# Top-k attention and a channel mix on one core: both passes over a batch's heads in the same order, and the last store on another queue

## The chip, the core and the metric

The kernel runs on one core of one Trainium2 chip. The metric is device time in microseconds (us) of one execution; less is better. A core has five engines that run their own instruction streams: TensorE (PE, matrix products and turns of tiles), VectorE (DVE), ScalarE (ACT), GpSimd (POOL) and SyncE (SP, which here only issues transfers). They wait for each other through semaphores. Transfers are done by 16 DMA engines; an engine's queue only issues them, in order, so that a transfer that has to wait holds up all that stand behind it on that queue.

## The reference

```python
# q, k, v: [8 batches, 8 heads, 576 tokens, 64]
scores = matmul(q, k.T) / sqrt(64)
kth = 32nd largest score of each row
scores = where(scores >= kth, scores, -1e9)
attn = exp(scores - max); attn /= sum(attn) + 1e-9
x = (attn @ v), heads side by side           # [8, 576, 512]
x_prev = x, one token later, zero in front
xk = mu_k * x + (1 - mu_k) * x_prev
xr = mu_r * x + (1 - mu_r) * x_prev
k = relu(xk @ w_k)                           # 512 -> 1024
out = sigmoid(xr @ w_r) * ((k * k) @ w_v)    # 1024 -> 512
```

## The kernel before

**Work.** Attention goes by pairs of heads (`hp`, four to a batch) and by tiles of 128 rows of scores: tile `i` from 0 to 7 of a pair alternates between its two heads over the first 512 tokens, tile 8 holds the last 64 tokens of both heads. That is 36 tiles a batch and 288 in all. A tile is scored on TensorE, copied to `sc` by ScalarE, searched for its 32nd largest value by VectorE (`cand`, `top`) with help of ScalarE and GpSimd (`sg`), masked (`E`), turned (`et`, `el`) and multiplied with `v` ("weigh", L1047 and L1048). After each four tiles (and after tile 8) the inverse row sums are spread by GpSimd into the single buffer `ri` (L1061), turned by TensorE (L1065), copied back by ScalarE (L1071), and VectorE "places" the weighed rows times `ri` in `xT` (L1078, L1080). The channel mix goes through the 4608 tokens in 19 chunks of `SIZES`: GpSimd and ScalarE make `xd`, `xm`, `xh`, `xl` from `xT`, TensorE multiplies them with `w_k` ("hidden"), `w_r` ("gate") and `w_v` ("value", all of them L687 to L689), and the result in `eb` is stored (L1217).

**Passes.** A batch is visited in parts, so that the mix of its first tokens can begin early: the first pass takes tiles 0 to 3 of each pair, the second tiles 4 to 8 (the last batch has three passes: 0 to 3, 4 to 7, 8). `visits()` lists them. Where two neighbouring visits are of the same pair, they are made one. Each visit loads the rest of the keys (`tl`), the queries (`qn`) and the values (`v`, `vr`, `vr8`), each of `tl`, `v`, `vr` and `vr8` into one buffer, so that a load waits for the last reader of the visit before. The keys of the first 512 tokens (`K`) are loaded and turned on a pair's first visit and kept: `K` has `1 + HOLD` = 4 buffers.

**Order.** Nothing is ordered by hand. Every step becomes an operation with a due time (`key`: the number of its tile, or the chunk's start, plus a constant from `OFF`) and a rough cost; `Plan.run` goes forward in a time of its own and lets the engine that can start first take, of the operations that are nearly ready, the one with the least due time. The order that comes out is fixed in the program. A small change of the graph can so exchange operations far from it. The weights are loaded as 20 blocks of 512 KB (L1246; those of `w_k` into `stage`, four buffers) in the time of the first 20 tiles, and unpacked by ScalarE and VectorE (L1247 to L1263), also between tiles.

**End.** After its last operation each engine reads a flag (L1339), branches past a second, exact version of the kernel that does not run here (L1345), and goes through closing semaphores (L1345, L1408). SyncE closes one semaphore for each lane of its transfers.

Of the kernel before, what the change touches and what calls it, by code (L numbers as in the profile page):

```python
# [26 lines left out]
HP = H // 2  # L27
# [16 lines left out]
           store=4.14, w=20.061, wabs=-2.342, wclamp=0.949, wshift=-6.042, wsign=-2.057, wexp=-2.168, wfine=1.502, whi=3.775, wmul=5.552,  # L44
           wsub=-10.606, wlo=3.473, spread=1.98, sliver=-2.472, low=4.289, lowt=-10.047, lowr=-8.942, lowc=-1.374)
CANDS, BESTS = 0.043, -0.709
LAG, STEP, WAT, WSTEP, GATE, VALUE, PACE = 10.811, 15.812, 2.487, 0.785, 7.769, 14.051, -2.0
HOLD = 3
HALVES = range(4), range(4, 9)
EDGE = {B - 1: (range(4), range(4, 8), range(8, 9))}  # L50

# [1 line left out]
def visits():  # L53

    vs = []
    for b in range(B):
        for k, part in enumerate(EDGE.get(b, HALVES)):
            for hp in range(HP)[::-1] if k % 2 else range(HP):
                if vs and vs[-1][:2] == (b, hp):
                    part = range(vs.pop()[2][0], part[-1] + 1)  # L60
                vs.append((b, hp, part))
                part = EDGE.get(b, HALVES)[k]
    return vs


VISITS = visits()
SIZES = [256] * 15 + [192, 256, 192, 128]
EVAC = 0, "et"
# [9 lines left out]
LWAT, LWSTEP = -2.585, 1.51  # L78
LAG0, LAG1 = 8.92, 22.884
WPE = 12  # L80
HEAD, TAIL = {}, {}
EARLY, LATE = 48, 252
LOOK = 16
WHOLE = "tk", "tq", "tr", "turn", "turni"
FULL = "sc", "K", "kd", "et", "el", "sg", "qs", "xm", "r", "eb", "lb", "ri"
MORE = dict(xh=2, xl=2, et=3, top=3, el=2, qn=2, K=1 + HOLD)

# [79 lines left out]
class Plan:  # L167
# [8 lines left out]
    def buf(self, name):  # L176
        return Buf(self.kinds[name])
# [225 lines left out]
def topk_attention_channel_mix(ctx: ExitStack, tc: tile.TileContext, q, k, v, mu_k, mu_r, w_k, w_v, w_r, out):  # L403
    nc = tc.nc
# [281 lines left out]
    def three(ps, sh, sl, mh, ml, first, last):  # L686
        return [nc.tensor.matmul(ps, lhsT=sh, rhs=mh, start=first, stop=False),  # L687
                nc.tensor.matmul(ps, lhsT=sh, rhs=ml, start=False, stop=False),  # L688
                nc.tensor.matmul(ps, lhsT=sl, rhs=mh, start=False, stop=last)]  # L689
# [160 lines left out]
    def new_batch(g):  # L850
        x = g.two.tile([128, HP, 1 + S], F32, name="xT")
        nc.gpsimd.memset(x[:, :, 0:1], 0.0)
        return x

    def attend(plan, visits, X, pair_sums):
        PE_, ACT, DVE, POOL, SP = plan.LANES
        starts = [0]
# [4 lines left out]
        units, seen, held = {}, None, {}  # L862

        for p, (b, hp, part) in enumerate(visits):
            P = Env()
            P.first = part[0]
# [5 lines left out]
            if fresh:  # L872
                P.kn, P.K = buf("kn"), buf("K")
            if any(x[:2] == (b, hp) for x in visits[p + 1:p + 1 + 2 * HOLD]):
                held[b, hp] = P.K
# [220 lines left out]
    def mixes(plan, xT, ready, tiles_all, X):  # L1096
        PE_, ACT, DVE, POOL, SP = plan.LANES
# [8 lines left out]
        chunks, t0 = [], 0  # L1106
        for size in SIZES:
            pieces, o = [], t0
            while o < t0 + size:
                b, s = divmod(o, S)  # L1110
                m = min(S - s, t0 + size - o)
# [7 lines left out]
        def piece(name, key, n, f, reads, writes):  # L1119
            cost = n  # L1120
            after = [last[0]] if last[0] else []
            o = plan.op(PE_, name, key, cost, cost + 180, f, reads=reads, writes=writes, mode="R", after=after, pace=min(key + PACE, tiles_all))
            last[0] = o
            return o

        at, size = 0, 0
        for c, (pieces, n, rows) in enumerate(chunks):
# [15 lines left out]
            for which in (0, 1):  # L1143
                xh, xl = C.x[which] = buf("xh"), buf("xl")
                k0 = key(0 if which == 0 else GATE)
                for i in range(2):
# [11 lines left out]
                    def add(i=i, xm=xm, offs=offs):  # L1158
# [4 lines left out]
                            reads=[xm], writes=[(xh, i)])  # L1163
                    plan.op(POOL, "xl" + "kr"[which], k0, 143 + 2.13 * 2 * n, 200 + 2.13 * 2 * n, lambda i=i, xm=xm, xh=xh, xl=xl, n=n: nc.gpsimd.tensor_sub(xl.t[:, 2 * i:2 * i + 2, :n], xm.t[:, :, :n], xh.t[:, 2 * i:2 * i + 2, :n].bitcast(F32)),
                            reads=[xm, (xh, i)], writes=[(xl, i)])
            hh, hl = buf("hh"), buf("hl")
            xh, xl = C.x[0]
            for f in range(0, NFB, 2):
# [6 lines left out]
                k1 = key(f + 1)  # L1175

                def relu(ph=ph, rr=rr, n=n):
# [7 lines left out]
                        reads=[rr, (hh, f)], writes=[(hl, f)], after=X.staged)  # L1185
            xh, xl = C.x[1]
            C.g = {}
            for t in range(0, n, 128):
                m = min(128, n - t)
                G = C.g[t] = Env()  # L1190
# [5 lines left out]
                k1 = key(GATE + 1 + t // 64)  # L1196
# [5 lines left out]
            for t in range(0, n, 128):  # L1202
                m = min(128, n - t)
                G = C.g[t]
                pv = buf("rot")
                for part in range(4):
                    def val(t=t, m=m, part=part, pv=pv, hh=hh, hl=hl):
                        return [y for f in range(part * NFB // 4, (part + 1) * NFB // 4) for y in three(pv.t[:m], hh.t[:, f, t:t + m], hl.t[:, f, t:t + m], wv[0][:, f, :], wv[1][:, f, :], f == 0, f == NFB - 1)]
                    piece("value", key(VALUE + t // 32 + part), 6 * 231, val, [(hh, 2 * part), (hl, 2 * part), (X.w["v"], (2 * part, 0)), (X.w["v"], (2 * part + 1, 0))], [pv])
                k1 = key(VALUE + 3 + t // 32)  # L1210
                if c == len(chunks) - 1:
                    plan.op(DVE, "scaled", k1, 586, 694, lambda G=G, m=m: nc.vector.scalar_tensor_tensor(G.e.t[:m], G.e.t[:m], 2.0, G.l.t[:m], op0=OP.subtract, op1=OP.mult), reads=[G.l], writes=[G.e])
                    plan.op(DVE, "gated", k1, 586, 694, lambda G=G, m=m, pv=pv: nc.vector.scalar_tensor_tensor(G.e.t[:m], G.e.t[:m], -1.0, pv.t[:m], op0=OP.mult, op1=OP.mult), reads=[pv], writes=[G.e])
                else:
                    plan.op(DVE, "scaled", k1, 586, 694, lambda G=G, m=m, pv=pv: nc.vector.scalar_tensor_tensor(pv.t[:m], G.l.t[:m], -1.0, pv.t[:m], op0=OP.mult, op1=OP.mult), reads=[G.l], writes=[pv])
                    plan.op(DVE, "gated", k1, 586, 694, lambda G=G, m=m, pv=pv: nc.vector.scalar_tensor_tensor(G.e.t[:m], G.e.t[:m], 2.0, pv.t[:m], op0=OP.subtract, op1=OP.mult), reads=[pv], writes=[G.e])
                plan.op(SP, "store", k1, 600, 2500, lambda G=G, m=m, t=t, rows=rows: nc.sync.dma_start(rows[t:t + m], G.e.t[:m]), reads=[G.e])  # L1217

    def weights(plan, X):
        PE_, ACT, DVE, POOL, SP = plan.LANES  # L1220
# [47 lines left out]
    def pipeline(stack):  # L1268
# [37 lines left out]
        def graph():  # L1306
            plan = Plan()
            for name, (tiles, banks, free) in made.items():
                plan.kind(name, len(tiles), banks, free)
                plan.kinds[name].tiles = tiles  # L1310
            X = Env()
            X.ranks, X.least, X.mu = plan.buf("ranks"), plan.buf("least"), plan.buf("wmu")
            def consts_in():
                return [nc.vector.tensor_copy(X.ranks.t[:, :9], ranks_i), nc.vector.memset(X.ranks.t[:, 9:10], -SCALE), nc.vector.memset(X.ranks.t[:, 10:11], BELOW)]
            plan.op("DVE", "ranks", -9, 250, 350, consts_in, writes=[X.ranks])
            plan.op("SP", "mu", 1.0, 1100, 2900, load_mu, writes=[X.mu])
            plan.op("DVE", "nmu", 3.0, 80, 183, lambda: nc.vector.tensor_scalar(nmu, mu, -1.0, 1.0, op0=OP.mult, op1=OP.add), writes=[X.mu])
            weights(plan, X)
            mixes(plan, *attend(plan, VISITS, X, pair_sums), X)
            return plan  # L1320
# [24 lines left out]
    with tc.If(again > 0):  # L1345
        with tc.For_i(0, B, 1) as b, ExitStack() as stack:
# [7 lines left out]
            rows = out[bass.ds(b, 1)].rearrange("o s d -> (o s) d")  # L1354
# [57 lines left out]
```

## Time and profile before

| | |
|---|---|
| median of 3 runs | 1287.63 us (1286.77 to 1289.1) |
| the profiled execution | 1288.26 us |
| its span, first to last instruction | 1286.4 us |
| TensorE busy | 1212.4 us, 94% |
| VectorE busy | 1139.6 us, 89% |
| ScalarE busy | 1115.1 us, 87% |
| GpSimd busy | 987.3 us, 77% |
| DMA, mean | 47 GB/s, 60.08 MB |
| granted TensorE clock, mean | 0.973 |

A share over the whole span hides the stages. The granted clock is 1.00 for nearly all of the time after the first 150 us (2.4 GHz) and 0.50 (1.2 GHz) in stretches before that, in one near 220 us and in one near the end of the attention.

### The profile page before, as it was taken

The numbers are of one execution on the slowest core, as the hardware profiler recorded it, in microseconds if no ns is written. First come the engines' busy times: TensorE is split into PE (matmuls) and PEld (weight loads), VectorE is DVE, ScalarE is ACT, GpSimd is POOL, SyncE is SP. The second block draws the span as 40 slices with busy tenths as digits, with TensorE's granted clock in tenths as the row PEclk, the third lists the DMA queues.
The fourth block names the chain that finished last, engine by engine and source line by source line (L and its number), as shares of the span: only waits on it lengthen the run. The fifth ranks groups of instructions, "written<-read, shape, count | busy, mean of one in ns | idle before, by whom it ended". The sixth has DMA issues, their size and how long they took to land.

```text
span 1286.4 us, 29892 instructions
## 1 busy us (share of the span) xinstructions
PE 1212.4 (94%) x9196; PEld 927.0 (72%) x9196; DVE 1139.6 (89%) x6219; ACT 1115.1 (87%) x2446; POOL 987.3 (77%) x885
## 2 busy tenths in 40 slices
PE   5876899999999999999999999999999999998996
PEld 2444676877777777777677777777778777776885
DVE  5999999999999999999999999999899999997110
ACT  5887898999999999999999989998989899997441
POOL 2559986887779868978698878887979778888583
PEclk8987799999999999999999999999999999999999
DMA  6233012111220112011211121112110111011000
GB/s 171 97 95 90 28 36 61 37 30 35 57 53 25 49 45 61 21 44 39 67 30 35 29 70 39 33 27 63 42 49 21 50 41 47 16 40 31 24 18 24
DMA packets 122090, 60.08 MB, mean 47 GB/s; under 512 B 99648, under 2 KB 114752, under 8 KB 121920
## 3 DMA queue, kind: packets, MB, share of 16 engines
q1 hardware_dynamic: 121376, 57.95, 16.9%
q8 instruction: 75, 1.23, 0.4%
q14 instruction: 95, 0.78, 0.2%
q10 hardware_dynamic: 544, 0.13, 0.0%
HBM read 48.60 MB, written 9.44 MB: 45 GB/s over the span
## 4 chain that ended last, share of the span: by engine, by line
PE 57%; ACT 18%; DVE 14%; POOL 4%; issue 1%; DMA 1%; SPq 0%; POOLq 0%; ACTq 0%; DVEq 0%
PE rot L687 10%; PE rot L689 9%; PE rot L688 9%; PE ps L1047 7%; PE rot L1017 6%; PE ps L971 6%; ACT sg L1001 3%; DVE cand L981 3%; ACT sc L976 3%; ACT se L1009 3%; DVE E L1012 3%; ACT et L1019 2%; DVE top L1004 2%; PE ps L967 2%; PE ps L1048 2%; PE ps L958 1%
## 5 line engine op out<-in xcount | busy, mean ns | idle before, releaser
L1003 POOL TENSOR_TENSOR sg<-sc,sg 128x576 f32<-128x576 f32 x288 | 409.9, 1425 | 183.3 <-ACT sg L1001 181.4
L981 DVE MAX8 cand<-sc 128x8 f32<-128x82 f32 (+1 forms) x2016 | 390.9, 232 | 11.7 <-ACT sc L976 10.5
L1001 ACT ACTIVATE sg<-sc,seen 128x576 f32<-128x576 f32 x288 | 226.4, 786 | 9.7 <-DVE seen L993 8.0
L1012 DVE SCALAR_TENSOR_TENSOR E<-sc,seen,se 128x576 f32<-128x576 f32 x288 | 231.2, 803 | 1.3 <-PE rot L1017 0.6
L1009 ACT ACTIVATE se<-sc,seen 128x576 f32<-128x576 f32 x288 | 217.6, 756 | 12.6 <-DVE E L1012 6.2
L1004 DVE MAX8 top<-sg 128x8 f32<-128x576 f32 x288 | 215.9, 750 | 12.5 <-POOL sg L1003 12.2
L976 ACT ACTIVATE sc<-ps 128x576 f32<-128x576 f32 x288 | 185.6, 657 | 33.6 <-PE ps L971 13.1
L1017 PE MATMUL rot<-ident,E 128*128 128x128 f32 x1152 | 182.9, 283 | 16.0 <-DVE E L1012 5.5
L1019 ACT ACTIVATE et<-rot 128x512 f32<-128x512 f32 x288 | 174.2, 606 | 13.1 <-PE rot L1017 10.6
L687 PE MATMUL rot<-xh,wk 128*128 128x256 f32 (+2 forms) x608 | 180.3, 297 | 2.1 <-ACT et L1019 1.1
L983 DVE MAX8 top<-cand 128x8 f32<-128x56 f32 x864 | 180.0, 208 | 2.4
L1017 PEld LDWEIGHTS rot<-ident,E 128*128 128x128 f32 x1152 | 132.7, 143 | 68.5 <-issue 7.8
L1047 PEld LDWEIGHTS ps<-et,v 128*64 128x64 f32 x2560 | 130.6, 140 | 58.6 <-ACT el L1028 20.0
L1047 PE MATMUL ps<-et,v 128*64 128x128 f32 (+1 forms) x2560 | 166.5, 274 | 4.3 <-ACT el L1028 3.5
L689 PE MATMUL rot<-xh,wk 128*128 128x256 f32 (+2 forms) x608 | 170.2, 280 | 0.0
L688 PE MATMUL rot<-xl,wk 128*128 128x256 f32 (+2 forms) x608 | 170.1, 280 | 0.0
L971 PE MATMUL ps<-K,qs 64*128 64x512 f32 x512 | 150.3, 665 | 0.0
L687 PE MATMUL rot<-wv,hh 128*128 128x512 f32 (+1 forms) x296 | 127.1, 429 | 2.5 <-ACT et L1019 2.3
L687 PEld LDWEIGHTS rot<-xh,wk 128*128 128x128 f32 x608 | 115.8, 191 | 8.3 <-ACT et L1019 2.3
L689 PE MATMUL rot<-wv,hl 128*128 128x512 f32 (+1 forms) x296 | 117.2, 396 | 0.0
L688 PE MATMUL rot<-wv,hh 128*128 128x512 f32 (+1 forms) x296 | 116.4, 393 | 0.0
L986 DVE MATCH_REPLACE8 cand<-top,cand 128x56 f32<-128x56 f32 x576 | 116.0, 201 | 0.0
(114 smaller groups left out, 2758.5 us busy)
## 6 DMA issues: line engine op xcount, KB each, us to landing
v<-in_v SPq DMA_DIRECT2D x59, 256.0 KB, 2.8
out<-eb SPq DMA_DIRECT2D x35, 256.0 KB, 2.2
kn<-in_k SPq DMA_DIRECT2D x64, 128.0 KB, 2.8
qn<-in_q SPq DMA_DIRECT2D x126, 64.0 KB, 2.1
stage<-in_moe_w_k SPq DMA_DIRECT2D x8, 512.0 KB, 5.5
xT<-in_moe_w_v SPq DMA_DIRECT2D x8, 512.0 KB, 3.7
xT<-in_moe_w_r SPq DMA_DIRECT2D x4, 512.0 KB, 6.4
tl<-in_k SPq DMA_DIRECT2D x118, 16.0 KB, 2.0
```

The lines of the kernel that those rows point to most:

```text
L687: return [nc.tensor.matmul(ps, lhsT=sh, rhs=mh, start=first, stop=False), nc.tensor.matmul(ps, lhsT=sh, rhs=ml, start=False, stop=False), ...
L688: nc.tensor.matmul(ps, lhsT=sh, rhs=ml, start=False, stop=False),
L689: nc.tensor.matmul(ps, lhsT=sl, rhs=mh, start=False, stop=last)]
L971: return [nc.tensor.matmul(ps[h].t, lhsT=qs.t[w, c * 128:(c + 1) * 128], rhs=P.K.t[w], start=True, stop=True) for h, w in enumerate(ws)]
L981: lambda T=T, c=c: nc.vector.max(T.cand.t[:, 8 * c:8 * c + 8], T.sc.t[:, CUTS[c]:CUTS[c + 1]]), reads=[T.sc], writes=[(T.cand, c)])
L1001: lambda T=T, sn=sn: nc.scalar.activation(T.side.t, T.sc.t, AF.Sign, bias=sn(T, 1), scale=-BELOW, accum_out=T.top.t[:, TOPK:TOPK + 1]),
L1003: plan.op(POOL, "below", n, 1375, 1430, lambda T=T: nc.gpsimd.tensor_mul(T.side.t, T.sc.t, T.side.t), reads=[T.sc], writes=[T.side])
L1004: plan.op(DVE, "eighth", n, 660, 754, lambda T=T: nc.vector.max(T.top.t[:, 24:32], T.side.t), reads=[T.side], writes=[(T.top, 3)])
L1009: plan.op(ACT, "exps", n, 667, 754, lambda T=T, pe=pe, sn=sn: nc.scalar.activation(pe.t, T.sc.t, AF.Exp, bias=sn(T, 0), scale=SCALE), read ...
L1012: lambda T=T, U=U, pe=pe, sn=sn: nc.vector.scalar_tensor_tensor(T.e(), T.sc.t, sn(T, 2), pe.t, op0=OP.is_ge, op1=OP.mult, accum_out=U.rs.t ...
L1017: return [nc.tensor.transpose(pt.t[:, c * 128:(c + 1) * 128], E.t[:, o + c * 128:o + (c + 1) * 128], ident) for c in range(NKC)]
L1047: return [*[nc.tensor.matmul(pa[hs[j]], lhsT=vs[j][:, c, :], rhs=ms[c][j], start=(c == 0), stop=False) for c in range(NKC) for j in range(2)],
```

## The change

`visits()` gets a flag `BACK`, False. Before, the second pass went through the pairs backwards (0 1 2 3, then 3 2 1 0), so that the visit at the turn was one visit of nine tiles; now both passes go 0 1 2 3. The turned keys of all four pairs are kept in the four buffers. Seven batches have eight visits in place of seven and the last has twelve in place of ten: 68 in place of 59. The order of tile kinds (`i`) is the same as before; the pairs that they belong to are not. Further, the due time of one mixing step (`addr`, the GpSimd addition L1160 for the gate) is 0.777 tiles earlier for due times past 252, and the last of the 36 stores of results is an operation of ScalarE's queue.

```diff
-HOLD = 3
+BACK, HOLD = False, 3
...
     for b in range(B):
         for k, part in enumerate(EDGE.get(b, HALVES)):
-            for hp in range(HP)[::-1] if k % 2 else range(HP):
+            for hp in range(HP)[::-1] if BACK and k % 2 else range(HP):
...
-HEAD, TAIL = {}, {}
+HEAD = dict()
+TAIL = dict(addr=-0.777)
...
-                plan.op(SP, "store", k1, 600, 2500, lambda G=G, m=m, t=t, rows=rows: nc.sync.dma_start(rows[t:t + m], G.e.t[:m]), reads=[G.e])
+                end = c == len(chunks) - 1 and t + 128 >= n
+
+                def store(G=G, m=m, t=t, rows=rows, issue=nc.scalar if end else nc.sync):
+                    issue.dma_start(rows[t:t + m], G.e.t[:m])
+                plan.op(ACT if end else SP, "store", k1, 600, 2500, store, reads=[G.e])
```

In the programs the changed kernel has on TensorE 9 more turns of `tl` (100 for 91), on ScalarE 9 more copies of them (`kd`, 128x128) and the store, on SyncE 9 more loads of `v`, 16 more of `vr` and 18 more of `tl`. All else is the same in number. VectorE's and GpSimd's instructions are the same; their order is not.

SyncE's queue at the start of the program, as it was: `kn` are keys, `tl` the rests of keys and queries, `vr_in` the rest of `v`, `stage` the blocks of `w_k`.

```order
14 L890 DMA qn_92<-in_q 128x2x64 x2
15 L881 DMA kn_91<-in_k 128x4x64 x2
16 L909 DMA vr_in<-in_v 64x2x64
17 L1246 DMA stage<-in_moe_w_k 128x1024
18 L897 DMA tl_94<-in_k 64x64 x2
19 L897 DMA tl_94<-in_q 64x64 x2
20 L1246 DMA stage<-in_moe_w_k 128x1024
21 L881 DMA kn_91<-in_k 128x4x64 x2
22 L1246 DMA stage<-in_moe_w_k 128x1024 x2
```

The same place of the changed program (its lines are a few numbers higher):

```order
14 L891 DMA qn_92<-in_q 128x2x64 x2
15 L882 DMA kn_91<-in_k 128x4x64 x2
16 L1251 DMA stage<-in_moe_w_k 128x1024 x2
17 L898 DMA tl_94<-in_k 64x64 x2
18 L1251 DMA stage<-in_moe_w_k 128x1024
19 L882 DMA kn_91<-in_k 128x4x64 x2
20 L1251 DMA stage<-in_moe_w_k 128x1024
21 L910 DMA vr_in<-in_v 64x2x64
```

The fourth visit is no longer the one of nine tiles, so its rest of the queries and its `vr8` are not due yet; two blocks of `w_k` stand directly behind the keys, and the third is separated from them by two loads.

GpSimd at the end of the attention, as it was: `ri` are the spreads of the last tiles 8 (`rs_121`, `rs_122`, ...), `sg_114` belongs to the last tile, `eb` are steps of the gate, `xm` and `xl` of the mix.

```order
822 L1061 TENSOR_SCALAR ri_130<-rs_121 128x128
823 L1198 TENSOR_SCALAR eb_141<-eb_141 64x512
824 L1201 TENSOR_TENSOR eb_143<-eb_143,lb_146 128x512
825 L1201 TENSOR_TENSOR eb_141<-eb_141,lb_144 64x512
826 L1003 TENSOR_TENSOR sg_114<-sc_107,sg_114 128x576
827 L1160 TENSOR_TENSOR xm_133<-xm_133,xT_148 128x512
828 L1160 TENSOR_TENSOR xm_134<-xm_134,xT_148 128x512
829 L1164 TENSOR_TENSOR xl_138<-xm_133,xh_136 128x512
830 L1164 TENSOR_TENSOR xl_138<-xm_134,xh_136 128x512
831 L1061 TENSOR_SCALAR ri_130<-rs_122 128x128
```

And now:

```order
822 L1062 TENSOR_SCALAR ri_130<-rs_121 128x128
823 L1004 TENSOR_TENSOR sg_114<-sc_107,sg_114 128x576
824 L1202 TENSOR_TENSOR eb_143<-eb_143,lb_146 128x512
825 L1199 TENSOR_SCALAR eb_141<-eb_141 64x512
826 L1062 TENSOR_SCALAR ri_130<-rs_122 128x128
827 L1161 TENSOR_TENSOR xm_133<-xm_133,xT_148 128x512
828 L1202 TENSOR_TENSOR eb_141<-eb_141,lb_144 64x512
829 L1165 TENSOR_TENSOR xl_138<-xm_133,xh_136 128x512
830 L1161 TENSOR_TENSOR xm_134<-xm_134,xT_148 128x512
831 L1151 TENSOR_TENSOR xd_131<-xT_148 128x2x192
832 L1062 TENSOR_SCALAR ri_130<-rs_123 128x128
```

The spread for `rs_122` stands ahead of the two additions and the two `xl` steps, no longer behind them.

## Rows read from the trace of the kernel before

**Rows 1.** Stretches: window, length, busy PE, PEld, DVE, ACT, POOL; clock, DMA.
```profile
50.00:140.00 90.00, 65.47 (x349) 38.16 (x348) 88.50 (x395) 78.39 (x161) 64.30 (x53) 0.81 0.28 80
140.00:1150.00 1010.00, 993.84 (x7890) 770.99 (x7891) 974.94 (x5493) 939.66 (x2079) 817.00 (x723) 1.00 0.16 41
...
1210.00:1276.50 66.50, 66.50 (x406) 56.95 (x404) 5.52 (x8) 25.97 (x55) 46.81 (x47) 1.00 0.05 15
```

**Rows 2.** Waits from 20 to 31.5 us: total, times, longest.
```profile
DVE rot L1248 <- ACT rot L1247: 5.0, 3, 2.2
```

**Rows 3.** Timeline of SyncE's queue: start, duration, transfer.
```profile
18.19 0.59 SPq L1246 DMA_DIRECT2D stage<-in_moe_w_k  x1
...
21.33 0.58 SPq L1246 DMA_DIRECT2D stage<-in_moe_w_k  x1
...
23.31 1.09 SPq L1246 DMA_DIRECT2D stage<-in_moe_w_k  x2
```

**Rows 4.** Timeline of ScalarE at the same place; idle before, and releaser, in brackets.
```profile
26.38 0.63 ACT L1247 ACTIVATE rot<-stage 128x512 f32<-128x512 f32 x1 [1.37 <-DMA stage<-in_moe_w_k]
...
30.18 0.62 ACT L1247 ACTIVATE rot<-stage 128x512 f32<-128x512 f32 x1 [1.95 <-DMA stage<-in_moe_w_k]
```

**Rows 5.** Timeline of TensorE: two turns of `tl` and what follows.
```profile
1168.81 0.38 PE L929 MATMUL rot<-ident,tl 128*128 128x128 f32 x2
1169.12 0.44 PE L1047 MATMUL ps<-et,v 128*64 128x128 f32 x4
```

**Rows 6.** Groups by line, shapes apart: count, busy us, mean ns, idle before.
```profile
L931 ACT ACTIVATE kd<-rot 128x128 f32<-128x128 f32 x27 | 7.5, 279 | 1.0 <-PE rot L929 0.9
```

**Rows 7.** Transfers by line, whole span: count, size, median us to landing.
```profile
v<-in_v SPq DMA_DIRECT2D x59, 256.0 KB, 2.8
```

**Rows 8.** Timeline of SyncE's queue and of TensorE: `v` and its first reader.
```profile
638.45 1.07 SPq L902 DMA_DIRECT2D v<-in_v  x1
...
642.51 1.09 PE L1047 MATMUL ps<-et,v 128*64 128x128 f32 x16
```

**Rows 9.** Timeline of TensorE at the end of the attention.
```profile
1185.98 0.40 PE L689 MATMUL rot<-wv,hl 128*128 128x512 f32 x1
1189.21 0.48 PE L1065 MATMUL rot<-ident,ri 128*128 128x128 f32 x1 [2.83 <-POOL ri L1061]
```

**Rows 10.** Timeline of GpSimd at the same place.
```profile
1177.45 0.30 POOL L1061 TENSOR_SCALAR ri<-rs 128x128 f32<-128x128 f32 x1
1177.83 1.91 POOL L1198 TENSOR_SCALAR eb<-eb 64x512 f32<-64x512 f32 x1
...
1182.60 1.42 POOL L1003 TENSOR_TENSOR sg<-sc,sg 128x576 f32<-128x576 f32 x1
1183.99 2.33 POOL L1160 TENSOR_TENSOR xm<-xm,xT 128x512 f32<-128x512 f32 x2
1186.29 2.48 POOL L1164 TENSOR_TENSOR xl<-xm,xh 128x512 fp32r<-128x512 f32 x2
1188.85 0.30 POOL L1061 TENSOR_SCALAR ri<-rs 128x128 f32<-128x128 f32 x1
```

**Rows 11.** Timeline of VectorE at the same place.
```profile
1185.53 0.22 DVE L1080 TENSOR_TENSOR xT<-ps,ri 128x64 f32<-128x64 f32 x1
```

**Rows 12.** A stretch with the half clock; columns as in rows 1.
```profile
1188.40:1195.20 6.80, 5.46 (x32) 3.48 (x33) 1.58 (x6) 2.53 (x7) 4.08 (x6) 0.50 0.12 42
```

**Rows 13.** Timeline of SyncE's queue: the last store.
```profile
1278.48 0.33 SPq L1217 DMA_DIRECT2D out<-eb  x1
```

**Rows 14.** Line L1345: duration ns min/median/max, first and last start us.
```profile
L1345 SPq EVENT_SEMAPHORE  x8: 17/17/17, 1282.3 to 1285.0; - x8
...
L1345 ACTq COMPARE_BRANCH  x1: 50/50/50, 1275.0 to 1275.0; - x1
...
L1345 ACTq EVENT_SEMAPHORE  x1: 17/17/17, 1277.7 to 1277.7; - x1
```

**Rows 15.** Waits of SyncE's queue over the span: total, times, longest.
```profile
SPq L1345 <- SPq L1345: 4.7, 2, 2.5
```

## The prediction

> **What bounds the kernel now.** I read the stretches first. From 50 to 140 us VectorE is busy for 88.5 of 90 us and TensorE for 65.5: no mix chunk is ready, and tiles come as fast as VectorE searches them and unpacks weights. From 140 to 1150 us TensorE is busy for 993.8 of 1010 us, and from 1210 to 1276.5 us for all 66.5 [rows 1]. So the path to the end is VectorE in the head, then TensorE. Three places with idle time on that path are left: VectorE's waits at the first weight blocks, TensorE's wait at the end of the attention, and the end of the program, where TensorE is done and others close up. The change touches all three. Everywhere else its price is the work that it adds to TensorE.
>
> **The head.** Between 20 and 31.5 us VectorE waits three times, 5.0 us together, for ScalarE's first step on a block of `w_k` [rows 2], and ScalarE waits for the block itself: 1.37 us at the second, 1.95 at the third [rows 4]. SyncE issues the three at 18.19, 21.33 and 23.31 us [rows 3]; in between stand the rest of the queries and keys of the next visits. In the new order the second block stands directly behind the first, so it is issued at about 18.8, 2.5 us sooner, and the third after two `tl` loads, at about 20.5, 2.8 us sooner. Upper bound: both of ScalarE's waits go, 3.3 us. Lower bound: the wait only moves, or ScalarE, which now has the second block's step ahead of a `sc` copy, holds that copy up; a loss of one such wait, 1.4 us. Two blocks that follow each other share the DMA engines, so the second will not land 2.5 us sooner; I take **-1.5 us**. VectorE has the same work up to tile 20, so this passes on to the start of the mix.
>
> **Nine more visits.** Each has one more turn of `tl` on TensorE. Two of them hold up the next instruction by 1169.12 - 1168.81 = 0.31 us [rows 5], so nine cost 9 x 0.155 = **+1.4 us**, all of it on the path. ScalarE gets nine more copies of 279 ns [rows 6], 2.5 us spread over 1100; it has gaps between its steps (939.7 of 1010 us busy [rows 1]), so I count nothing, and 2.5 us as the upper bound should each hold up a tile. The nine loads of `v` land within 2.8 us (median) [rows 7]. They are hidden because the first weigh of a visit stands behind two tiles of that visit (one tile for a tile 8); at the tightest place that I found, the load is issued at 638.45 (1.07 us) and read at 642.51 [rows 8], and TensorE shows no wait there: 4.06 us, of which 2.8 and the issue leave 0.2. If this cover is gone, TensorE stands still for what is lacking. The rest of the order on TensorE, scores, turns, weighs and mix, is mixed anew in small steps: by tile 288 it has as many mix matmuls behind it as before, and in between, looked at after each twelfth tile, the new program is never more than 24 of them ahead or behind. I count 0 for it with bounds of 3 us either way, which is a fifth of the 16.2 us that it is idle from 140 to 1150 [rows 1].
>
> **The end of the attention.** TensorE's last value matmul starts at 1185.98, then it waits for 2.83 us for GpSimd's `ri` and goes on at 1189.21 [rows 9]. GpSimd made the first of these spreads at 1177.45. Then came gate steps from 1177.83 to 1182.60, `sg` of the last tile, two additions (2.33) and two `xl` steps (2.48), and the next spread at 1188.85 [rows 10]. None of these is needed before it; what it does need is that VectorE has placed the rows before it, since `ri` is one buffer: 1185.53 + 0.22 = 1185.75 [rows 11]. In the new order only `sg` and part of the gate steps stand ahead of it: 1177.75 + 1.42 + at most 4.77 (all the gate steps) = 1183.9, under 1185.75. So the spread starts at about 1185.9 and ends at 1186.2, when TensorE's matmuls end too (1185.98 + 0.4 = 1186.4): the 2.83 us go nearly whole. Right behind that wait the granted clock was 0.50 from 1188.40 to 1195.20, with TensorE busy for 5.46 us of it [rows 12]; at the full clock the same work takes half, 2.7 us less. If the clock stays up without the wait, both together are 5.5 us. What GpSimd now does later, the additions and `xl`, is read by the hidden matmuls some 10 us on, so they have room. I take **-4.4 us**: some of a stall of this size comes back as smaller ones, since the chain spread, turn, copy, place, spread runs once for each of the four last tiles. Bounds: -2 (part of the wait goes, the clock falls all the same) and -6.
>
> **The last store.** SyncE issues it at 1278.48 (0.33 us) [rows 13]. Only then does it read the flag and branch, and its eight closing semaphores run from 1282.3 to 1285.0 [rows 14], with two waits for nothing but itself, 4.7 us together, the longer 2.5 [rows 15]: one from the branch to the first semaphore, one of 2.2 among the eight. So after the second, at about 1284.6, 1.8 us are left to the end of the span (1286.4). Without the last store SyncE has nothing to wait for after the store before it, and it can branch and fill its queue long before. ScalarE takes the wait over: 1278.5 + 0.3 for the issue + 0.5 to 0.9 for flag and branch + 2.7 from branch to its one closing semaphore (1275.0 to 1277.7 [rows 14]) = 1282.2. With the same 1.8 us of closing the span ends at 1284.0 or, as some of SyncE's eight are already passed, a little sooner: -2.4 to -3.0. I take **-2.5 us**. Lower bound: -0.3.
>
> The Trainium skill ("Runtime: NRT & Kernel Launch", section "Instruction fetch mechanics") says that a taken branch whose target is not among the few blocks of instructions at hand makes the engine fetch them before it goes on. SyncE's two waits for itself agree with that. By that rule ScalarE, which now branches after the last store, pays in SyncE's place.
>
> **Sum.** -1.5 + 1.4 - 4.4 - 2.5 = -7.0 us. The profiled execution took 1288.26 us, so 1281.3 by it; it lies 0.63 over the median of 1287.63, against which I put the number: **1280.6 us**, 0.5% less. A difference under 0.2% (2.6 us) can hardly be told from none here.
>
> **Rivals.**
> (a) *Forecast*, chance 0.55: all three places give; with the bounds above 1277.5 to 1283.5.
> (b) *The wait at the end of the attention stays in another place* (a late turn, a late `v` for the tiles 8, the clock falls all the same), chance 0.15: -1.5 + 1.4 - 0.5 - 2.5 = -3.1, so 1284.5. For it: the chain of the four last tiles is a serial one, and the pair of tile 8 now needs a `v` of its own where it had the same as tiles 4 to 7. Against: it is one added load, and between the weigh that frees its buffer and its reader stand mix matmuls, as they do between the four tiles 8 now.
> (c) *The closing stall moves along with the store*, chance 0.10: if ScalarE waits twice as SyncE did, 4.7 us, then 1278.8 + 0.7 + 4.7 + 1.8 = 1286.0, a gain of 0.4 for 2.5; 1282.7 in all. Against: ScalarE's own wait after its branch was one of 2.7 us, and it closes one semaphore, not eight.
> (d) *The gains are eaten by the new order*, chance 0.11: the head gives nothing (0), ScalarE's copies count (+2.5), TensorE's new order costs 3: 0 + 1.4 + 2.5 + 3 - 4.4 - 2.5 = 0.0, so 1287.6.
> (e) *Slower: `v` comes too late in the added visits*, chance 0.09. SyncE's queue is in order, and a `v` that waits for the last weigh can itself stand behind `tl` and `qn` loads. The tightest place has 0.2 us to spare [rows 8]. From there on each microsecond by which SyncE is later is one by which TensorE stands still; with 1.5 us more at all nine added visits that is 9 x 1.3 = +11.7, and with the other terms 1280.6 + 11.7 = 1292.3.
>
> **Numbers.** The range reaches over (a), (b) and (c) and into (d): 1277.0 to 1286.8. Faster by over 0.2% (below 1285.05): (a) and (c) but for a little, two thirds of (b): 0.76. Slower by over 0.2% (above 1290.2): (e) but for a little, 0.08. The rest, 0.16, within 0.2%.
>
> **What would show it.** In the changed profile: VectorE's wait for ScalarE's first weight step near 20 to 31 us at 3.5 us or less; 100 turns of `tl`; no wait of TensorE for `ri` over 1 us at the end of the attention, and the clock at 1.00 there; the last store on ScalarE's queue, SyncE's two waits for itself ahead of it, and some 5.5 us from the store's issue to the end of the span in place of 7.9. Wrong would make it: a wait of TensorE for `v`, more than 19 us of idle TensorE from 140 to 1150 us, a new stall of VectorE in the head, or a fall of the clock in a place that has none now.

## The result, and the profile after

The changed kernel takes **1258.57 us** (median of 4 runs, 1257.0 to 1260.28), the kernel before 1287.85 beside it: a ratio of 0.9773 [0.9756, 0.979], 2.3% faster. The forecast was 1280.6 with a range of 1277.0 to 1286.8. The direction held, the size did not: 29 us for 7.

To see where they are, I cut each trace at five points of TensorE's stream that exist in every version: the last turn of `E` of tiles 20, 281 and 288 (there are four turns to a tile, 1152 in all, so the tiles can be counted), the start of the last matmul, and the end of the span. For the changed kernel the last of these turns is in the first row below; the second is the count of the `tl` turns (line numbers are 1 to 5 higher than before, and some 25 to 35 in e7, e8, e9 and e13).

```profile
L1018 PE MATMUL rot<-ident,E x1152: 270/273/476, 21.3 to 1176.2; 128*128 128x128 f32 x192
```

```profile
L930 PE MATMUL rot<-ident,tl 128*128 128x128 f32 x100 | 24.2, 292 | 1.6 <-ACT et L1020 1.1 <-DMA tl<-in_q 0.3
```

All kernels of this study, in us of their profiled execution (e is short for the experiments below; bold is what an experiment was made to move):

| kernel | to tile 20 | 20 to 281 | 281 to 288 | to last matmul | to end | span |
|---|---|---|---|---|---|---|
| before | 138.5 | 1018.0 | 43.9 | 75.8 | 10.2 | 1286.4 |
| **after** | 135.1 | 1005.2 | 36.0 | 75.8 | 6.4 | 1258.4 |
| e1 backward | 137.8 | 1017.9 | 43.1 | 75.8 | **6.8** | 1281.3 |
| e2 store on SyncE | 132.8 | 1005.0 | 36.0 | 75.8 | **7.8** | 1257.4 |
| e3 forward, moved | 133.5 | **1018.2** | 35.6 | 76.1 | 6.3 | 1269.7 |
| e5 spread late | 133.4 | 1005.2 | **40.5** | 75.8 | 6.5 | 1261.5 |
| e6 turns twice | 135.7 | **1012.4** | 36.5 | 75.8 | 6.3 | 1266.8 |
| e7 spread early | 140.5 | 1017.6 | **44.4** | 75.8 | 6.8 | 1285.1 |
| e8 blocks early | **134.2** | 1017.9 | 44.0 | 75.8 | 6.9 | 1278.8 |
| e9 blocks sooner | **137.6** | 1005.1 | 36.0 | 75.8 | 6.3 | 1260.8 |
| e10 backward, refit | 136.8 | **1008.2** | 36.1 | 76.1 | 6.4 | 1263.7 |
| e11 forward, moved more | 132.5 | **1012.6** | 38.4 | 75.8 | 6.3 | 1265.5 |
| e12 backward, moved more | 136.9 | **1016.4** | 37.3 | 75.8 | 6.5 | 1273.0 |
| e13 spread, copy early | 139.9 | 1017.3 | **44.9** | 75.4 | 6.9 | 1284.3 |

From before to after: head -3.4, middle -12.8, end of the attention -7.9, closing -3.8; together -27.9 of the span's -28.0. The largest part lies in the middle, where I had counted nothing.

The cut at tile 281 does not part equal work: in the changed kernel 12 matmuls of the mix fewer stand between tiles 281 and 288 than before, as they are done ahead of tile 281. From tile 20 to tile 288 the work is the same but for the nine visits: 1061.9 us before, 1041.2 after, 1053.8 in e3, 1051.0 in e11, 1053.7 in e12 and 1044.3 in e10. (e10 has done 24 matmuls of the mix ahead of tile 20; at the mean of 0.125 us a matmul that is an estimated 3 us of work less in its sum.)

The stretches of the changed kernel, to hold against [rows 1]:

```profile
50.00:140.00 90.00, 68.49 (x371) 41.68 (x372) 89.11 (x396) 79.12 (x163) 65.29 (x54) 0.79 0.28 83
140.00:1120.00 980.00, 971.86 (x7779) 759.29 (x7779) 958.37 (x5421) 926.91 (x2060) 808.09 (x715) 1.00 0.17 44
1150.00:1180.00 30.00, 28.79 (x231) 21.21 (x230) 16.94 (x76) 20.69 (x51) 25.13 (x25) 1.00 0.18 53
1180.00:1246.00 66.00, 66.00 (x441) 57.60 (x440) 5.75 (x9) 26.56 (x56) 46.48 (x48) 1.00 0.05 15
```

TensorE stood idle for 16.2 of 1010 us before and for 8.1 of 980 now. These two stretches do not hold the same work. From tile 20 to tile 252 they do (2280 matmuls of the mix in both kernels); the row before and the row after:

```profile
138.53:1045.60 907.07, 893.21 (x7121) 693.09 (x7120) 878.01 (x4952) 843.50 (x1866) 732.90 (x652) 1.00 0.16 42
135.08:1029.92 894.84, 886.01 (x7124) 693.17 (x7124) 875.41 (x4954) 845.58 (x1880) 733.27 (x652) 1.00 0.17 45
```

Of the 12.2 us that went here, 5.0 were idle time (13.9 to 8.8) and 7.2 were busy time, for the same number of matmuls. So about half of the gain lay within the busy rows. That these were short waits between matmuls is inferred from the counts, not shown one by one. The split is good to some 2 us: e1, with the order of before, takes the same 907 us with 16.1 of them idle.

The clock was at 1.00 in the third row, where [rows 12] had 0.50.

VectorE's waits for the first weight steps, to hold against [rows 2], and SyncE's queue there, against [rows 3]:

```profile
DVE rot L1253 <- ACT rot L1252: 2.7, 2, 2.0
```

```profile
17.57 1.09 SPq L1251 DMA_DIRECT2D stage<-in_moe_w_k  x2
18.75 1.48 SPq L898 DMA_DIRECT2D tl<-in_k  x2
20.27 0.75 SPq L1251 DMA_DIRECT2D stage<-in_moe_w_k  x1
...
23.02 0.80 SPq L1251 DMA_DIRECT2D stage<-in_moe_w_k  x1
```

The end of the attention, TensorE and then GpSimd, against [rows 9] and [rows 10]: GpSimd stands idle for 0.22 us until VectorE has placed the rows, the spread follows, and its turn follows a value matmul without a wait.

```profile
1166.35 0.40 PE L690 MATMUL rot<-wv,hl 128*128 128x512 f32 x1
1166.58 0.27 PE L1066 MATMUL rot<-ident,ri 128*128 128x128 f32 x1
1167.39 0.27 PE L1092 MATMUL rot<-ident,least 128*1 128x128 f32 x1 [0.54 <-ACT ri L1072]
```

```profile
1165.77 0.30 POOL L1062 TENSOR_SCALAR ri<-rs 128x128 f32<-128x128 f32 x1 [0.22 <-DVE xT L1081]
```

The closing, against [rows 13] and [rows 14]: ScalarE issues the last store, then branches; SyncE branched 18 us before.

```profile
1253.93 0.37 ACTq L1221 DMA_DIRECT2D out<-eb  x1
```

```profile
L1350 SPq EVENT_SEMAPHORE  x8: 17/17/17, 1239.7 to 1256.9; - x8
L1350 SPq COMPARE_BRANCH  x1: 50/50/50, 1237.1 to 1237.1; - x1
L1350 ACTq COMPARE_BRANCH  x1: 54/54/54, 1254.9 to 1254.9; - x1
L1350 ACTq EVENT_SEMAPHORE  x1: 17/17/17, 1257.5 to 1257.5; - x1
```

### The profile page after: what moved, and what is told of

The parts are those of the page before. It is cut to its first block, busy times and chain, and to the rows that moved or that the text cites. A ratio compares the mean times of both kernels' runs of the same rounds, so it can differ in the third digit from the quotient of the medians.

```text
span 1258.4 us, 29994 instructions
## 1 busy us (share of the span) xinstructions
PE 1204.9 (96%) x9205; PEld 926.6 (74%) x9205; DVE 1136.3 (90%) x6219; ACT 1114.2 (89%) x2455; POOL 986.4 (78%) x885
## 4 chain that ended last, share of the span: by engine, by line
PE 70%; ACT 12%; DVE 11%; issue 1%; POOL 1%; DMA 0%; POOLq 0%; DVEq 0%; ACTq 0%
PE rot L688 12%; PE rot L690 11%; PE rot L689 11%; PE ps L1048 9%; PE rot L1018 8%; PE ps L972 8%; DVE cand L982 2%; ACT sg L1002 2%; ACT sc L977 2%; ACT se L1010 2%; PE ps L968 2%; PE ps L959 2%; DVE E L1013 2%; PE ps L1049 2%; PE rot L917 2%; ACT et L1020 1%
## 5 line engine op out<-in xcount | busy, mean ns | idle before, releaser
L1018 PEld LDWEIGHTS rot<-ident,E 128*128 128x128 f32 x1152 | 132.8, 143 | 60.2 <-issue 6.5
L688 PE MATMUL rot<-wv,hh 128*128 128x512 f32 (+1 forms) x296 | 125.9, 425 | 0.5 <-ACT ri L1072 0.4
L689 PEld LDWEIGHTS rot<-xl,wk 128*128 128x128 f32 x608 | 116.0, 191 | 0.1
```

The lines of the kernel that those rows point to most:

```text
L1018: return [nc.tensor.transpose(pt.t[:, c * 128:(c + 1) * 128], E.t[:, o + c * 128:o + (c + 1) * 128], ident) for c in range(NKC)]
```

## The experiments

**Theories.** *Order*: the gain of the middle and of the end belongs to the one order of steps that the planner now writes; other due-time constants lose it with both passes forward, and others find it with a backward pass. *Direction*: going forward itself takes the waits away. Beside these stood the closing, and the single steps of my sum. The kernels e1, e7, e8, e10, e12 and e13 run the second pass backward and have the last store on ScalarE's queue; in the others both passes run forward. e7, e8, e9 and e13 edit the finished order: `rows[lane]` is one engine's list of steps, and the lists are merged again so that every engine keeps its own. All kernels of the experiments keep the constant of `addr`, and none has both passes forward without it. It moves due times past 252 tiles, so the 12.2 us that went up to tile 252 lie ahead of what it moves; how much of the 8.5 behind that is due to it, no run shows. e4, a further backward order with moved constants, has no time.

**e1_backward**

```diff
-BACK, HOLD = False, 3
+BACK, HOLD = True, 3
```

> The changed kernel with its second pass run backward again, the last store still on ScalarE's queue: what the end of the program alone is worth. The closing in the changed kernel came out 3.8 us shorter than before, and the order of the steps on every other engine is here that of the kernel before. If the gain beyond the closing comes from the order of steps that the forward pass brings (the order theory, and the direction theory too): 1287.9 - 3.8 = about 1284, between 1283 and 1286. If the store's move did more than close the program sooner (rival: it frees SyncE's queue or the DMA engines earlier on): below 1278.

Measured 1283.2 us, ratio 0.9971 [0.9958, 0.9983]. The store alone is worth some 4 us; head, middle and end stand as before. TensorE, VectorE, ScalarE and GpSimd run the same sequence of operations as before the change, so with a backward pass the constant of `addr` moves nothing.

**e2_store_on_sp**

```diff
-                end = c == len(chunks) - 1 and t + 128 >= n
+                end = False
```

> The changed kernel with its last store back on SyncE's queue, both passes forward. The order of all else stays. The span of the changed kernel's closing was 3.8 us shorter than before, so 1258.6 + 3.8 = 1262.4; my forecast had 2.5 for it: 1261.1. If nearly all of the gain hung on the store: above 1275. SyncE should wait for itself twice behind the last store, 4 to 5 us together, as it did before the change.

Measured 1259.63, 0.9787 [0.9771, 0.9803], 1.1 us over the changed kernel by the medians, and 1.4 by the closing. SyncE waited for itself once, not twice:

```profile
SPq L1350 <- SPq L1350: 2.6, 1, 2.6
```

So this expectation failed by more than half, 1.1 to 1.4 us for 2.5 to 3.8: with the longer SyncE program of the forward pass (43 loads more) the second of the two waits [rows 15] is gone although the store is back. Backward, the move of the store is worth 3.4 us of closing; forward, 1.4.

**e3_forward_due_moved**

```diff
+import random as _r
+_r.seed(6)
+OFF = {k: x + _r.uniform(-0.005, 0.005) for k, x in OFF.items()}
```

> The changed kernel, both passes forward, the same steps and the same number of each, but every due-time offset moved by a random amount of at most 0.005 tiles, which makes the planner choose another order of the same steps on every engine. Order theory (the gain is that this one order of steps, which the offsets happen to fit, leaves TensorE fewer small waits): most of the middle's and the attention's end's gain is lost, 1270 to 1280. Direction theory (going forward, keeping the keys turned and with them an earlier first half of the mix's inputs, is what removes the waits, whatever the order): the gain stays, 1257 to 1262.

Measured 1271.61, 0.9875 [0.9858, 0.9891]. Head and end are as after the change (133.5, 35.6), the middle is back at 1018.2: by this cut all 13 us of it are gone with the same steps, the same loads and the same direction. Some of that is work moved over the cut, as e3 has 12 matmuls of the mix more behind it at tile 281 than the changed kernel; from tile 20 to 288 it has lost 12.6 of the 20.7 us. Direction theory, by which the gain stays whatever the order, falls. TensorE's row from 140 to 1120 us:

```profile
140.00:1120.00 980.00, 965.93 (x7711) 751.83 (x7710) 948.34 (x5370) 919.28 (x2043) 797.53 (x706) 1.00 0.17 44
```

It got through 7711 matmuls in 980 us, the changed kernel through 7779, e1 through 7678.

**e10_backward_refit**

```diff
+OFF.update({'kt': -21.7909, 'kq': -11.0286, 'rest': -13.4112, 'v': -2.5946,
...
 'lowt': -10.0402, 'lowr': -8.9375, 'lowc': -1.375})
```

(82 constants, moved by 0.04 in the median, by 0.29 at most.)

> The second pass backward and nine visits merged, as before the change, the last store on ScalarE's queue, and the due-time offsets sought anew for this pass (all of them moved, most by less than 0.1, until the planner's order had fewer gaps). Order theory: backward has orders as good, and this one keeps most of the 24.6 us by which the forward kernel is ahead of the backward one with the old offsets (1283.2): 1262 to 1272. Direction theory: a backward pass keeps its waits in the middle, so the head and the end of the attention alone can be mended: 1274 or more.

Measured 1266.43, 0.9847 [0.9831, 0.9864]: the middle takes 1008.2, the end 36.1. By constants alone a backward pass is 16.8 us faster than e1, and faster than the forward e3.

**e11_forward_moved_more** and **e12_backward_moved_more**

```diff
+import random as _r
+_r.seed(1)
+OFF = {k: x + _r.uniform(-0.05, 0.05) for k, x in OFF.items()}
```

(and `BACK` True in the second)

> The changed kernel, both passes forward, with every offset moved at random by at most 0.05 tiles (ten times as far as in e3_forward_due_moved). Order theory: another order, another place for small waits; 1264 to 1280, as e3_forward_due_moved was 1271.6. Direction theory: under 1262.

> The same moved offsets as in e11_forward_moved_more, with the second pass backward and nine visits merged; last store on ScalarE's queue. Order theory: it too lies in 1264 to 1284, and the difference to e11_forward_moved_more, of either sign, is smaller than the 24.6 us between the two directions with the old offsets: at most 10. Direction theory: 20 us or more over e11_forward_moved_more.

Measured 1267.56, 0.9859 [0.9842, 0.9875], and 1275.01, 0.9915 [0.9898, 0.9932]. The difference is 7.4 us, 4.4 of it in the head; the middle differs by 3.8. With the old constants the two directions lie 24.6 apart. Forward is ahead here too, so a share of a few us for the direction itself is not excluded.

**e8_blocks_early**: e1 with SyncE's head as after the change.

```diff
+    row = rows["SP"]
+    row[13:20] = [row[i] for i in (14, 16, 15, 18, 17, 19, 13)]
```

> The backward kernel with the last store on ScalarE's queue (1283.2 us in the first group), and the head's order moved on SyncE alone: the second and third block of w_k, and the small load of v, stand where they stand after the change; all other engines keep the backward order. My forecast had 1.5 us for this: 1281.7. In the runs with the forward pass tile 20 came 3.4 to 5.7 us sooner than before: if the blocks' issue is all of that, 1277.5 to 1280, and VectorE's three waits for the first weight steps fall from 5.0 to 2 to 3 us. If it is the order on the other engines: above 1282.5.

Measured 1279.85, 0.9932 [0.9916, 0.9949], 3.4 us under e1; tile 20 at 134.2, 3.6 sooner. VectorE's waits from 20 to 31.5 us:

```profile
DVE rot L1277 <- ACT rot L1276: 1.5, 1, 1.5
```

The order of SyncE's loads there (two blocks earlier, the small load of `v` later) brings the whole head term, and it is more than the 1.5 that I had for it.

**e9_blocks_sooner**: the changed kernel, both blocks one place further ahead.

```diff
+    first = [o for o in row if o.name == "w"][:2]
+    at = row.index(first[0])
+    row[at - 1:at + 2] = [*first, row[at - 1]]
```

> The changed kernel with the first two blocks of w_k one place further ahead on SyncE's queue, ahead of the keys of the visit that they stood behind; all other engines keep their order. VectorE still waits there for 2.0 to 2.7 us for ScalarE's first weight steps, and ScalarE for the blocks (0.78 and 0.79). If the issue of the blocks still sets the head: 1 to 2 us sooner, 1256.6 to 1257.6. If the keys that now come 1 us later hold up tiles in turn: no change or up to 2 us later.

Measured 1261.68, 0.9805 [0.9789, 0.9821], so 3 us slower, at tile 20 by 2.5. ScalarE's timeline says why: the copy of `K` stands ahead of the first weight step, and waits for the turn of the keys that are now behind the blocks. TensorE's row of that turn, then ScalarE's:

```profile
23.82 1.08 PE L943 MATMUL rot<-ident,kn 128*128 128x128 f32 x4 [6.68 <-DMA kn<-in_k]
```

```profile
26.29 0.59 ACT L948 ACTIVATE K<-rot 128x512 f32<-128x512 f32 x1
26.77 1.18 ACT L1278 ACTIVATE rot<-stage 128x512 f32<-128x512 f32 x2
```

After the change that turn ran at 20.46, the copy at 22.93 and the first weight step at 24.31. The place after the change is better than the one on either side of it.

**e6_turns_twice**

```diff
-... for i in range(m)]
+... for i in range(m) for _ in range(2)]
```

> The changed kernel with every turn of tl on TensorE made twice: 100 turns more, the same values written over. It enlarges the price of the added visits' turns elevenfold. By my forecast's 0.155 us a turn, all on the path: +15.5 us, about 1274. If the turns fill waits of TensorE instead (rival: that is why the nine added ones were not to be seen): under +7, below 1266.

Measured 1267.13, 0.9835 [0.9819, 0.9852]: 8.6 us for 100 turns by the medians, 7.8 for the 90 of them from tile 20 to 288. A turn costs 0.09 us, not 0.155, and nine of them 0.8. That lies between the two expectations: the turns do not just fill waits, but each takes less than the two in [rows 5].

**e5_spread_late**

```diff
-return nc.gpsimd.tensor_scalar(to, r, 1.0, 1.0, op0=OP.mult, op1=OP.mult)
+return [nc.gpsimd.tensor_scalar(to, r, 1.0, 1.0, op0=OP.mult, op1=OP.mult)
+        for _ in range(12 if late else 1)]
```

(`late`: last batch, tile 8, second pair)

> The changed kernel, with the next to last but one spread of the attention (the one for which TensorE waited before the change) written twelve times over by GpSimd, 0.30 us each, so that it ends 3.3 us later; nothing else is edited or moved. In the run after the change the end of the attention, from tile 281 to tile 288, came 7.9 us sooner than before. If the late spread was the cause of all of it: 5.5 to 8 us come back, 1264 to 1267. If it was worth what my forecast had for it, wait and clock together: 4.4 us, about 1263. If it was worth its wait alone, and the rest came from how the steps around it stand: 2.5 to 3.3 us, 1261 to 1262, with the granted clock at 1.00 behind the wait.

Measured 1263.4, 0.9811 [0.9791, 0.9831]: 4.8 us more, 4.5 of them from tile 281 to 288. TensorE's wait, and the stretch behind it, where the clock falls to the lower level:

```profile
PE rot L1066 <- POOL ri L1062: 3.6, 1, 3.6
```

```profile
1169.70:1173.20 3.50, 3.50 (x11) 1.99 (x10) 1.57 (x6) 1.31 (x3) 3.50 (x4) 0.51 0.00 0
1173.20:1180.00 6.80, 6.80 (x69) 4.82 (x68) 1.16 (x3) 3.86 (x10) 5.14 (x7) 1.00 0.18 43
```

One late spread, with the fall of the clock, is worth about what I had for it (4.4). That it comes so close is in part luck: its wait is 3.6 us in place of 2.83, and the half clock lasts 3.5 us in place of 6.8.

TensorE's rows from tile 281 to tile 288, before, after and in e5, tell what the end's 7.9 us are:

```profile
1156.54:1200.42 43.88, 38.86 (x275) 28.62 (x273) 25.92 (x132) 29.06 (x69) 32.36 (x30) 0.92 0.11 30
1140.27:1176.24 35.97, 34.67 (x262) 25.71 (x261) 25.09 (x124) 28.61 (x68) 30.01 (x29) 1.00 0.15 44
```

```profile
1138.64:1179.15 40.51, 36.29 (x262) 26.55 (x261) 25.23 (x124) 28.66 (x68) 33.33 (x40) 0.96 0.15 39
```

From before to after idle time fell by 3.7 us (5.0 to 1.3) and busy time by 4.2. Of the busy time some 2.7 are the half clock of [rows 12] (half of 5.46), and the 1.5 left go with the 12 matmuls of the mix that stand ahead of tile 281 now. In e5 2.9 of idle time and 1.6 of busy time come back.

**e7_spread_early**: e1 with this spread put ahead of the additions and `xl` steps on GpSimd.

```diff
+    row = rows["POOL"]
+    late = [o for o in row if o.name == "spread"][-3]
+    at = row.index(late)
+    row.insert(at - 4, row.pop(at))
```

> The backward kernel with the last store on ScalarE's queue (1283.2 us in the first group), and one step moved on GpSimd alone: the spread for which TensorE waited at the end of the attention stands ahead of the two additions and the two xl steps, as after the change; all other engines keep the backward order. My forecast had 4.4 us for this: 1278.8, with the wait of 2.8 us gone and the clock at 1.00. If the spread was the cause of all that the end of the attention gained: 7.9 us, 1275.3. If the wait only moves to the next step of the chain: 0 to 1 us, above 1282.

Measured 1285.99, 0.9985 [0.9974, 0.9995]: nothing gained, the end takes 44.4. The rows of TensorE's waits, GpSimd and ScalarE:

```profile
PE rot L1118 <- ACT ri L1098: 2.6, 1, 2.6
```

```profile
1188.45 0.30 POOL L1088 TENSOR_SCALAR ri<-rs 128x128 f32<-128x128 f32 x1 [2.94 <-DVE xT L1107]
```

```profile
1189.84 0.63 ACT L1189 ACTIVATE xh<-xm 128x512 fp32r<-128x512 f32 x1 [3.82 <-POOL xm L1187]
1191.06 0.63 ACT L1189 ACTIVATE xh<-xm 128x512 fp32r<-128x512 f32 x1 [0.59 <-POOL xm L1187]
1191.60 0.26 ACT L1055 ACTIVATE el<-ps 128x128 f32<-128x128 f32 x1
1191.76 0.43 ACT L1098 ACTIVATE ri<-rot 64x64 f32<-64x64 f32 x2
```

GpSimd now stands still for 2.94 us with the additions behind the spread; ScalarE's `xh` steps wait for these, and the copy of `ri` stands behind `xh`. The wait moved from GpSimd to ScalarE.

**e13_spread_and_copy_early**: e7, and on ScalarE `el` and `ri` ahead of the two `xh`.

```diff
+    row = rows["ACT"]
+    copy = [o for o in row if o.name == "ri"][-3]
+    at = row.index(copy)
+    row[at - 3:at + 1] = [*row[at - 1:at + 1], *row[at - 3:at - 1]]
```

> The backward kernel with the last store on ScalarE's queue, the spread moved ahead on GpSimd as in e7_spread_early, and on ScalarE the copies of el and ri ahead of the two xh steps, as after the change (in e7_spread_early the xh steps waited 3.82 us for GpSimd's additions, and TensorE 2.65 us for the ri copy behind them). From tile 281 to tile 288 the backward kernel took 43.1 us, e7_spread_early 44.4, the changed kernel 35.9, e5_spread_late 40.6. If GpSimd's and ScalarE's order together carry the end's gain: 36 to 40 us for that stretch, no wait of TensorE over 1 us in it, the clock at 1.00, and 1276 to 1280 in all. If TensorE's own order is needed too: 42 to 45 us for it, the wait moved once more, 1282 to 1286.

Measured 1286.13, 0.999 [0.9982, 0.9999]; the end takes 44.9. The wait moved once more, to the weigh that needs the next tile's `et`; that copy stands behind `xm` steps which wait for GpSimd. TensorE, then ScalarE:

```profile
1190.16 0.40 PE L720 MATMUL rot<-wv,hl 128*64 128x512 f32 x1
1194.60 0.69 PE L1078 MATMUL ps<-et,v 128*64 128x64 f32 x16 [4.04 <-ACT et L1050]
```

```profile
1192.34 1.58 ACT L1186 ACTIVATE xm<-xd,nmu 128x192 f32<-128x192 f32 x4 [2.64 <-POOL xd L1181]
1193.95 0.60 ACT L1050 ACTIVATE et<-rot 128x512 f32<-128x512 f32 x1
```

In the changed kernel this `et` stands ahead of the `xm` steps:

```profile
1169.03 0.60 ACT L1020 ACTIVATE et<-rot 128x512 f32<-128x512 f32 x1 [0.87 <-PE rot L1018]
...
1171.90 0.79 ACT L1156 ACTIVATE xm<-xd,nmu 128x192 f32<-128x192 f32 x2
```

So one step moved on GpSimd and two on ScalarE are not enough, and the wait that is left is again one of ScalarE's order. Whether the whole orders of these two engines would do, or TensorE's own is needed too, no run shows. All orders but that of before (with e1) and its edits e7, e8 and e13 have an end of 35.6 to 38.4, backward ones too (and e5, the changed order with one late step, 40.5).

## Why the prediction was wrong

**The step that failed** is the sentence on TensorE's mixed order, "I count 0 for it with bounds of 3 us either way, which is a fifth of the 16.2 us that it is idle". It measured -12.8 by the cut at tile 281, and -12.2 up to tile 252, where the work is equal. Two things were wrong with it. The stock of waits was taken from the idle time beside the busy rows alone: only 5.0 of the 12.2 us came from there, and 7.2 from the busy time of as many matmuls. And the spread was a guess: six orders of all but the same work (before, after, e3, e10, e11, e12) put the middle at 1005.2 to 1018.2 us, 13 us apart, and tiles 20 to 288 at 1041.2 to 1061.9. The old order lies at the slow end of these and the new is the fastest; nothing in my working could tell that beforehand. A stretch at the half clock near 220 us, which the kernel before had, is not the cause: e1 has none there, and the same 1017.9.

**The head** (-1.5, bounds to -3.3): the mechanism held and e8 shows it alone; the size was -3.4 by the two profiles and by the medians of e8 and e1. The kernels with the new order on SyncE (after, e2, e5, e6, e8) reach tile 20 at 134.3 in the mean, those with the old one (before, e1, e7, e13) at 139.2, so it may be up to 5. I had reasoned that two blocks share the DMA engines and took under half; VectorE's waits fell by 2.3 to 3.5, and tile 20 came 3.4 to 3.6 sooner.

**Nine more visits** (+1.4): 0.8 by e6, for the turns alone. No wait of TensorE for `v` shows after the change, and the loads land in the same 2.8 us (median) as in [rows 7], 68 of them now; rival (e) did not come. What ScalarE's copies cost by themselves, no run shows.

```profile
v<-in_v SPq DMA_DIRECT2D x68, 256.0 KB, 2.8
```

**The end of the attention** (-4.4, bounds to -6): -7.9. Of that 1.5 is work moved ahead of tile 281, and 6.4 are waits and the half clock, where I had 5.5 for both and took off 1.1 for what would come back as smaller waits. In sum nothing came back: idle time there fell by 3.7, more than the one wait of 2.83. But the argument, that GpSimd's additions and `xl` have room when they come later, was made for GpSimd's order alone, and e7 shows that in the old order of the other engines they have none: rival (b) came true there, twice over (e13). The gain came with the new order on several engines at once; which of their steps it needs is open.

**The last store** (-2.5): the closing is 3.8 us shorter, 3.4 in e1. By e2 the move of the store is worth 1.4 of the 3.8 with both passes forward; the other 2.4 came with the forward program even with the store on SyncE. From the issue to the end of the span 4.5 us passed where I expected 5.5 and [rows 13] had 7.9, as SyncE had passed six of its eight semaphores by 1240.1 and only 0.9 us were left behind ScalarE's, not 1.8. ScalarE went from branch to semaphore in 2.6 us, once, not twice as in rival (c). By the rule that I named (the Trainium skill, "Runtime: NRT & Kernel Launch", section "Instruction fetch mechanics": a taken branch to instructions that are not at hand stalls the engine) ScalarE pays one stall; the 2.6 us agree with one. That e2 lost one of SyncE's two stalls by a longer program would fit the same rule, but no run here shows where the blocks of instructions lie.

**What stays open**: which exchanges of steps make the middle's 12.8 us. Its waits are many and short (the largest sum by cause that the trace shows after the change is 1.1 us from 140 us on), and no edit of single steps was run there. A share of a few us for the direction is not excluded either.

## What to carry to other kernels

Where a planner orders the steps, a change of the graph draws a new order, and the order can be worth more than the change: before sizing such a change, time a few orders of the same work with slightly moved constants, and hold the change against their spread. Do not take the idle time of a 98% busy engine as what an order can win; compare its busy time over the same number of instructions too, and cut two traces where they have done the same work. A wait in a chain over four engines may give nothing back to one edit, as in e7: ask what stands behind each step that it makes wait.

## What was not expected of the hardware

The head varies between kernels with the same order of steps there: the turn of tile 20 stood at 132.8 to 135.7 us in the four forward kernels with the new order (after, e2, e5, and e6 with its turns doubled) and at 137.8 to 140.5 in the four with the old (before, e1, e7, e13). A single profile so can't size a head term below 3 us; the groups lie 5 apart. And the same last store on SyncE's queue closed the program 10.2 us after the start of the last matmul before the change and 7.8 after it in e2, with one wait of SyncE for itself of 2.6 in place of two of 4.7 together.
